# Score products of a sliding-window attention kernel at 128 columns where only 128 are read

## The chip, the cores and the metric

The kernel runs on one core of a Trainium2 chip. A core has TensorE (PE: matrix products; its weight loads are shown apart as PEld), VectorE (DVE), ScalarE (ACT), GpSimd (POOL) and SyncE (SP), which issues most transfers here. The metric is the time of one execution in device microseconds; lower is better.

## What is computed

The input has 2048 tokens of 512 values. Cut to what matters, with 32 heads of 16 values and a window of 256 tokens:

```
xn     = layernorm(x)
q,k,v  = split(xn @ wqkv)
scores = q @ k.T / 4, kept where 0 <= i - j < 256
s      = (softmax(scores) @ v) @ wo
g      = silu((silu(xn @ w_gate) * (xn @ w_up)) @ w_down)
out    = x + s * g
```

## The kernel before, in words

The tokens are worked in four chunks of 512. The dense products (projections `a`, values `vp`, gate and up `g`, `u`, down `d`, output `s`) split each fp32 operand into a high and a low part of type F32R (a 4-byte type that TensorE runs in its own way) and add three products, high by high, low by high and high by low. They contract over 64 rows at a time: the array is used as two halves, rows 0 to 63 and 64 to 127, and each half runs its own stream of products beside the other (`half(r)`).

Attention is worked in 32 units, 8 per chunk, each of four heads. In each unit the scores are computed twice:

- `max_pair` (line 955) makes a tile `b` for each of 16 pairs of head and block of 128 queries: queries by keys, 384 keys wide, or less in the first chunk, where the first two blocks of queries have only 128 and 256 keys behind them. VectorE (line 977) adds the mask and takes the maximum over the `n` columns that count. The product is `w` columns wide.
- `max_turn` turns the maxima, and they are added to the queries as one more row.
- `prob_pair` (line 1073) makes tiles `c`, keys by queries, in pieces that the function `pieces` lists. A piece is (key block, first query block, width `w`, first column in the bank `at0`, and the columns `v0` to `v1` of it that are used). ScalarE (line 1084) takes the exponential over the used columns, GpSimd masks the diagonal blocks.
- `pv_visit` (line 1140) multiplies the probabilities with the values on eight tiles of the array of 64 by 32. Its operands are plain F32, not F32R.

Here `b` and `c` have F32R operands (`qs` and `ks`), with 48 and 49 rows, one half of the array for each of two heads.

The order of the instructions of all engines is written out by a planner in the program: it keeps a clock for each half of TensorE (`issue`, line 1315, adds 0.000447 us per column and 0.004 us per product) and one for each other engine, and it puts attention work between dense products by due times that count finished dense work:

```
def issue(r, cols):
    front[0] = max(front[0], clock[r])
    clock[r] = front[0] + cols * 0.000447 + 0.004
```

On the chip the engines wait for one another by semaphores alone.

Of the kernel before, what the change touches and what calls it, by code (L numbers as in the profile page):

```python
# [54 lines left out]
def tile_window_attention_swiglu_gate(  # L55
# [27 lines left out]
    def sb(name, shape, dtype, kind, n):  # L83
        return pers.tile(shape, dtype, name=name, tag=ring(kind, n), bufs=1)
# [21 lines left out]
    def do(e, ready, cost, fn, then=None, slack=0.5, can=None, lat=None):  # L106
        seq[0] += 1
        queue[e].append((ready + slack, seq[0], ready, cost, fn, then, can, LAT.get(e, 0.0) if lat is None else lat))
# [67 lines left out]
    def bank(pool, name):  # L176
        tag = min((v, k) for k, v in pool.items() if v is not None)[1]
        pool[tag] = None
        return ps.tile([P, 512], F32, name=name, tag=tag, bufs=1), tag
# [775 lines left out]
    def max_pair(u, p, qb):  # L955
        c = u // NG
        lo = qb * P
        n = 3 * P
        if c == 0 and qb < 2:
            lo, n = HALO, (qb + 1) * P  # L960
        w = max(n, 256)
        m = mts[u % 2]
        for h in range(2):
            j = 2 * p + h
            r = R * h
            pb, tag = bank(rb_free, f"b{u}_{qb}_{j}")

            def go(pb=pb, r=r):
                nc.tensor.matmul(  # L969
                    pb[:, :w], qs[u % 3][r : r + 48, p, qb * P : (qb + 1) * P],  # L970
                    ks[u % 3][r : r + 48, p, lo : lo + w], start=True, stop=True,
                )

            def ttr(pb=pb, j=j):
                junk = sb(f"jk{u}_{qb}_{j}", [P, 3 * P], BF16, "jk", 1)
                col = 8 * (j % 2) + 4 * (j // 2) + qb
                nc.vector.tensor_tensor_reduce(  # L977
                    junk[:, :n], pb[:, :n], maskb[:, 3 * P - n :], 1.0, -3.0e38,
                    ALU.add, ALU.max, m[:, col : col + 1],
                )  # L980

            def after(t, tag=tag):
                rb_free[tag] = t
                ttr_at[u] = ttr_at.get(u, []) + [t]

            extra[h].append((w, go, lambda t, ttr=ttr, after=after: do("V", t, 0.23 + 0.00098 * n, ttr, after, 0.0)))
# [43 lines left out]

    def pieces(c, e):
        if c == 0:
            return ([(3, 2, 256, 0, 128, 256), (2, 2, 256, 256, 256, 512)],
                    [(0, 0, 384, 0, 0, 384)], [(1, 1, 384, 0, 0, 384)])[e]
        return ([(3, 2, 256, 0, 128, 256), (-2, 0, 256, 256, 256, 384)],
                [(-1, 0, 256, 0, 0, 256), (2, 2, 256, 256, 256, 512)],
                [(0, 0, 384, 0, 0, 384)], [(1, 1, 384, 0, 0, 384)])[e]

# [22 lines left out]
    def prob_span(u, e):  # L1061
        pcs = pieces(u // NG, e)
        return min(q[4] for q in pcs), max(q[5] for q in pcs)
# [9 lines left out]
    def prob_pair(u, e, p):  # L1073
        c = u // NG
        pcs = pieces(c, e)
        a, b = prob_span(u, e)
        if p == 0:
# [62 lines left out]
    def pv_visit(u, es):  # L1140
# [3 lines left out]
        for e in es:  # L1144
            for kb, qb, w, at0, v0, v1 in pieces(c, e):
                for r in range(2):
                    k64 = 2 * kb + r
                    a, b = max(k64, 0), min(k64 + 5, 8)
                    jobs[r].append((b - a, e, kb, R * a, R * b, at0 + R * a - P * qb))
# [57 lines left out]
    def plan_attention():  # L1207
        for u in range(NU):
            c = u // NG
            if u:  # L1210
                marks.append((u - 1 + 0.3, load_qk, (u,)))
            for n in range(8):
                streams[0].append((u + 0.02 + 0.1 * n, max_ready, max_pair, (u, n // 4, n % 4)))
            streams[0].append((u + 0.8, turn_ready, max_turn, (u, 0)))
            streams[0].append((u + 0.8, turn_ready, max_turn, (u, 1)))
            ne = 3 if c == 0 else 4
            for n in range(2 * ne):
                streams[1].append((u + 1.07 + 0.1 * n, prob_ready, prob_pair, (u, n // 2, n % 2)))
            streams[1].append((u + 1.89, pv_ready, pv_visit, (u, tuple(range(ne)))))
        for c in range(1, NCH):  # L1220
            marks.append((8 * c - 4.9, load_x, (c,)))
            for k in range(KC):
                streams[2].append((8 * c - 3.3 + 0.25 * k, xt_ready, xt_turn, (c, k)))
        for s in streams:
            s.reverse()
        marks.sort(key=lambda m: -m[0])
# [258 lines left out]
```

## Time and profile before

| | |
|---|---|
| time, median of 3 runs | 858.4 us (857.58 to 859.4) |
| time of the profiled execution | 858.88 us |
| its span, first to last instruction | 857.2 us |
| granted TensorE clock, mean | 0.999 |
| PE, PEld busy | 99%, 92% of the span |
| DVE, ACT, POOL busy | 57%, 58%, 70% of the span |

The time is the span and 1.7 us around it. A product's duration in the trace holds the time that it takes to pass through the array, so products that overlap are each shown longer than the distance between their starts. A busy TensorE is therefore not one at its peak; distances between starts say what a product costs.

### The profile page before, as it was taken

To read this page: it belongs to the slowest core of one execution; us is meant where nothing else is said; L and a number is where in the kernel's file an instruction comes from. 1 tells how busy PE (TensorE), PEld (TensorE's weight loads), DVE (VectorE), ACT (ScalarE), POOL (GpSimd) and SP (SyncE) were. 2 spreads that over 40 slices of the span, in tenths; PEclk is the share of its full clock that TensorE was granted. 3 is DMA by queue.
4 is the path that set the end of the run, shared out by engine and by line. 5 is a ranking of instruction groups with operands and counts; after the bars stand their busy time and mean duration, and the time that the engine had idled before them with its cause. 6 is when DMAs were issued, how large, how long until landed. Compare 5 with 4: busy or idle time off the path is not lost.

```text
span 857.2 us, 29679 instructions
## 1 busy us (share of the span) xinstructions
PE 851.1 (99%) x11960; PEld 792.0 (92%) x11960; DVE 485.9 (57%) x1633; ACT 495.9 (58%) x1056; POOL 597.3 (70%) x630
## 2 busy tenths in 40 slices
PE   9999999999999999999999999999999999999997
PEld 8999999999899898989899999899999989989897
DVE  4464566655656656755566755566556656554233
ACT  4445565555766566565576655555656765555632
POOL 6756565758885766666789685666658797769754
PEclk9999999999999999999999999999999999999999
DMA  5854645457667853455767686454656767634341
GB/s 177 218 163 140 198 119 173 132 161 176 181 170 208 267 146 112 134 155 130 209 171 198 188 205 182 122 164 113 179 128 176 200 181 233 170 98 137 101 138 63
DMA packets 67629, 139.59 MB, mean 163 GB/s; under 512 B 12690, under 2 KB 21394, under 8 KB 67492
## 3 DMA queue, kind: packets, MB, share of 16 engines
q1 hardware_dynamic: 67204, 137.17, 57.3%
q8 instruction: 94, 1.54, 0.8%
q10 hardware_dynamic: 288, 0.52, 0.2%
q14 instruction: 43, 0.35, 0.1%
HBM read 107.74 MB, written 29.62 MB: 160 GB/s over the span
## 4 chain that ended last, share of the span: by engine, by line
PE 97%; DMA 1%; DVE 1%; issue 0%; ACT 0%; SPq 0%; DVEq 0%; ACTq 0%
PE g L455 19%; PE u L455 18%; PE d L455 18%; PE a L455 11%; PE pv L1160 8%; PE c L1123 6%; PE s L455 5%; PE vp L455 5%; PE b L969 5%; PE warm L235 1%; DMA wr<-wdn 1%; PE xp L473 0%; DVE jk L977 0%; PE xp L340 0%; PE mt L1003 0%
## 5 line engine op out<-in xcount | busy, mean ns | idle before, releaser
L426 POOL TENSOR_TENSOR wl<-wr,wh 128x512 fp32r<-128x512 f32 x240 | 298.2, 1259 | 137.8 <-ACT wh L438 129.1
L977 DVE CUSTOM_DVE_ANT_0 jk<-b,maskb 128x384 bf16<-128x384 f32 (+2 forms) x512 | 271.4, 530 | 141.3 <-PE b L969 80.7
L1084 ACT ACTIVATE p<-c 128x384 f32<-128x384 f32 (+1 forms) x480 | 208.0, 498 | 93.0 <-PE c L1123 83.7
L455 PE MATMUL d<-wh,hh 64*128 64x256 f32 x1792 | 237.2, 279 | 0.0
L455 PEld LDWEIGHTS d<-wh,hh 64*128 64x128 f32 x1792 | 208.2, 186 | 1.3 <-issue 0.8
L455 PE MATMUL d<-wl,hh 64*128 64x256 f32 x896 | 190.8, 279 | 0.0
L438 ACT ACTIVATE wh<-wr 128x512 fp32r<-128x512 f32 x240 | 142.6, 620 | 81.6 <-PE u L455 24.7
L455 PE MATMUL g<-xh,wl 64*128 64x512 f32 x448 | 173.0, 395 | 0.5 <-issue 0.5
L455 PE MATMUL g<-xh,wh 64*128 64x512 f32 x448 | 173.1, 395 | 0.0
L455 PE MATMUL g<-xl,wh 64*128 64x512 f32 x448 | 173.0, 394 | 0.0
L455 PE MATMUL u<-xh,wl 64*128 64x512 f32 x448 | 171.9, 396 | 0.0
L455 PE MATMUL u<-xl,wh 64*128 64x512 f32 x448 | 171.2, 394 | 0.0
L455 PE MATMUL u<-xh,wh 64*128 64x512 f32 x448 | 171.2, 394 | 0.0
L455 PEld LDWEIGHTS d<-wl,hh 64*128 64x128 f32 x896 | 143.0, 186 | 0.3
L1097 POOL TENSOR_SCALAR_AFFINE_SELECT p<-p 128x512 f32<-128x512 f32 x128 | 81.1, 637 | 51.6 <-ACT p L1084 46.9
L969 PE MATMUL b<-k,q 48*128 48x384 f32 (+1 forms) x512 | 111.6, 334 | 0.0
L1123 PE MATMUL c<-q,k 49*128 49x384 f32 (+1 forms) x704 | 105.2, 304 | 0.1
L455 PE MATMUL a<-xh,wh 64*128 64x512 f32 (+1 forms) x264 | 90.4, 395 | 0.0
L455 PE MATMUL a<-xh,wl 64*128 64x512 f32 (+1 forms) x264 | 88.6, 386 | 0.0
L455 PE MATMUL a<-xl,wh 64*128 64x512 f32 (+1 forms) x264 | 88.3, 387 | 0.0
L455 PEld LDWEIGHTS g<-xl,wh 64*128 64x128 f32 x448 | 82.6, 186 | 2.9 <-issue 0.2
L455 PEld LDWEIGHTS g<-xh,wh 64*128 64x128 f32 x448 | 82.7, 186 | 2.6 <-issue 0.2
(102 smaller groups left out, 2020.5 us busy)
## 6 DMA issues: line engine op xcount, KB each, us to landing
wr<-wgu SPq DMA_DIRECT2D x56, 512.0 KB
k<-qkd SPq DMA_DIRECT2D x48, 192.0 KB
wr<-wqk SPq DMA_DIRECT2D x16, 512.0 KB
qkd<-qkh SPq DMA_DIRECT2D x32, 256.0 KB
qkd<-qkl SPq DMA_DIRECT2D x32, 256.0 KB
q<-qkd SPq DMA_DIRECT2D x64, 128.0 KB
wr<-wdn SPq DMA_DIRECT2D x16, 512.0 KB
od<-ev SPq DMA_DIRECT2D x32, 256.0 KB
```

The lines of the kernel that those rows point to most:

```text
L235: nc.tensor.matmul(wbank[:, : rhs.shape[-1]], warm, rhs, start=True, stop=True)
L426: nc.gpsimd.tensor_tensor(lo, raw[j][:, n], f32(hi), op=ALU.subtract)
L438: do("S", t, 0.13 + 0.00078 * m, lambda: nc.scalar.activation(hi, raw[j][:, n], AF.Copy), after_high, sl)
L455: return nc.tensor.matmul(pb, a, b, start=first, stop=last, skip_group_check=True)
L969: nc.tensor.matmul(pb[:, :w], qs[u % 3][r : r + 48, p, qb * P : (qb + 1) * P], ks[u % 3][r : r + 48, p, lo : lo + w], start=True, stop=True,)
L977: nc.vector.tensor_tensor_reduce(junk[:, :n], pb[:, :n], maskb[:, 3 * P - n :], 1.0, -3.0e38, ALU.add, ALU.max, m[:, col : col + 1],)
L1084: nc.scalar.activation(t[:, h, :], pc[:, a:b], AF.Exp, scale=DH ** -0.5)
L1097: nc.gpsimd.affine_select(s, s, [[0, 4], [1, P]], ALU.is_ge, 0.0, base=0, channel_multiplier=-1)
L1123: nc.tensor.matmul(pc[:, at0 : at0 + w], ks[u % 3][r : r + 49, p, k0 : k0 + P], qs[u % 3][r : r + 49, p, qb * P : qb * P + w], start=(i == ...
L1160: nc.tensor.matmul(pbs[r][0][32 * j : 32 * j + 32, q0:q1], vt[half(r), (4 * c + kb) % VT, VW * (4 * g + j) : VW * (4 * g + j) + 32], t[hal ...
```

## The change

The score products of which only 128 columns are read become 128 columns wide in place of 256. In `max_pair` that is the first block of queries in the first chunk. In `pieces` it is the piece of key block 3, which had computed query block 2 too and left it unread, and, from the second chunk on, that of key block -2. What is read, the number of products, their operands in SBUF and all other code stay. The planner is told the new widths, since `w` is what it gets.

```diff
@@ max_pair
-        w = max(n, 256)
+        w = n
@@ pieces
         if c == 0:
-            return ([(3, 2, 256, 0, 128, 256), (2, 2, 256, 256, 256, 512)],
+            return ([(3, 3, 128, 128, 128, 256), (2, 2, 256, 256, 256, 512)],
                     [(0, 0, 384, 0, 0, 384)], [(1, 1, 384, 0, 0, 384)])[e]
-        return ([(3, 2, 256, 0, 128, 256), (-2, 0, 256, 256, 256, 384)],
+        return ([(3, 3, 128, 128, 128, 256), (-2, 0, 128, 256, 256, 384)],
                 [(-1, 0, 256, 0, 0, 256), (2, 2, 256, 256, 256, 512)],
                 [(0, 0, 384, 0, 0, 384)], [(1, 1, 384, 0, 0, 384)])[e]
```

## Rows read from the trace of the kernel before

**Rows 1.** The page, its head and the busy time of TensorE.

```profile
span 857.2 us, 29679 instructions
...
PE 851.1 (99%) x11960; PEld 792.0 (92%) x11960; DVE 485.9 (57%) x1633; ACT 495.9 (58%) x1056; POOL 597.3 (70%) x630
```

**Rows 2.** The page, the chain that ended last, by engine and line.

```profile
PE 97%; DMA 1%; DVE 1%; issue 0%; ACT 0%; SPq 0%; DVEq 0%; ACTq 0%
PE g L455 19%; PE u L455 18%; PE d L455 18%; PE a L455 11%; PE pv L1160 8%; PE c L1123 6%; PE s L455 5%; PE vp L455 5%; PE b L969 5%; PE warm L235 1%; DMA wr<-wdn 1%; PE xp L473 0%; DVE jk L977 0%; PE xp L340 0%; PE mt L1003 0%
```

**Rows 3.** All waits: who waited for whom, us, times, longest us.

```profile
ACT p L1084 <- PE c L1123: 83.7, 98, 5.0
DVE jk L977 <- PE b L969: 80.7, 100, 4.2
```

**Rows 4.** The waits of TensorE's weight loads, same columns.

```profile
PEld pv L1160 <- issue: 4.9, 16, 0.4
PEld pv L1160 <- POOL p L1101: 2.2, 6, 0.4
...
PEld c L1123 <- ACT p L1084: 1.0, 4, 0.3
```

**Rows 5.** Groups by form, PE: xcount, busy us, mean ns, idle before.

```profile
L455 PE MATMUL g<-xh,wh 64*128 64x512 f32 x448 | 173.1, 395 | 0.0
...
L969 PE MATMUL b<-k,q 48*128 48x384 f32 x448 | 99.1, 341 | 0.0
...
L1123 PE MATMUL c<-q,k 49*128 49x384 f32 x256 | 53.8, 342 | 0.0
L1123 PE MATMUL c<-q,k 49*128 49x256 f32 x448 | 51.5, 283 | 0.1
...
L1160 PE MATMUL pv<-p,v 64*32 64x320 f32 x1024 | 41.8, 435 | 0.0
...
L1160 PE MATMUL pv<-p,v 64*32 64x128 f32 x448 | 13.4, 269 | 0.0
L969 PE MATMUL b<-k,q 48*128 48x256 f32 x64 | 12.4, 286 | 0.0
...
L1160 PE MATMUL pv<-p,v 64*32 64x64 f32 x448 | 11.2, 222 | 0.0
```

**Rows 6.** Timeline of PE, 405.3 to 407.5 us: start us, us, group.

```profile
405.41 0.41 PE L1123 MATMUL c<-q,k 49*128 49x256 f32 x4
405.65 0.40 PE L455 MATMUL a<-xl,wh 64*128 64x512 f32 x2
405.89 0.34 PE L969 MATMUL b<-k,q 48*128 48x384 f32 x2
406.07 0.40 PE L455 MATMUL a<-xh,wl 64*128 64x512 f32 x2
...
406.99 0.40 PE L455 MATMUL a<-xh,wh 64*128 64x512 f32 x2
407.23 0.40 PE L1123 MATMUL c<-q,k 49*128 49x256 f32 x4
407.47 0.40 PE L455 MATMUL a<-xl,wh 64*128 64x512 f32 x2
```

**Rows 7.** Timeline of PE, 401.3 to 403.5 us.

```profile
401.64 0.28 PE L455 MATMUL d<-wl,hh 64*128 64x256 f32 x2
...
403.35 0.28 PE L455 MATMUL d<-wl,hh 64*128 64x256 f32 x2
```

**Rows 8.** Groups by form, PEld (the weight loads).

```profile
L1123 PEld LDWEIGHTS c<-q,k 49*128 49x128 f32 x704 | 78.0, 186 | 4.7 <-ACT p L1084 1.0 <-DVE m L977 0.5
...
L1160 PEld LDWEIGHTS pv<-p,v 64*32 64x32 f32 x2816 | 50.3, 106 | 26.7 <-issue 4.9 <-POOL p L1101 2.2 <-DVE m L977 0.4
```

**Rows 9.** The longest pieces of the chain: start us, us, what.

```profile
399.11 2.38 PE pv L1160 x93
```

## The prediction

> **What bounds the kernel now.** I read the head of the page first, then the chain of work that ended last, then the waits, and only then single products. TensorE is busy for 851.1 of 857.2 us [rows 1]; that alone says little, since overlapping products are shown longer than they cost. The chain says more: 97% of the span is TensorE, and the lines that the change touches, `c` (L1123) and `b` (L969), hold 6% and 5% of it [rows 2]. The waits point the same way. The two readers of the scores sit idle until TensorE delivers: ScalarE 83.7 us for `c`, VectorE 80.7 us for `b` [rows 3], while the largest waits on TensorE's own side are a few us over the whole run [rows 4]. So nothing covers a score product: whatever one of them costs in its half of the array, more or less, goes into the time.
>
> **How many products change.** From the code: in `max_pair`, the first of four query blocks for 4 heads in the 8 units of the first chunk, 32 products. In `pieces`, one piece for 4 heads in those 8 units, 32, and two pieces for 4 heads in the 24 other units, 192. Together 256, all from 256 to 128 columns. The trace agrees with this reading of the code: it has 448 `c` of 256 columns (64 in the first chunk, 384 after) and 64 such `b` [rows 5]; half of each is to change. Two heads run side by side on the two halves, so 128 changes lie behind one another in each half. The price wanted is that of one product in its half, times 128.
>
> **What one costs now.** Distances between starts, not durations. Four `c` of 256 columns, two in each half, start at 405.41 and the next product at 405.65; again at 407.23 and 407.47 [rows 6]: 0.24 us for two, 120 ns each. Dense products of 256 columns: from 401.64 to 403.35 there are 15 in each half, 114 ns each [rows 7]. A `b` of 384 takes 0.18 us (405.89 to 406.07), and five products of 512 from 406.07 to 407.23, of which the last starts at 406.99, take 230 ns each (0.92 us over four) [rows 6]. So from 256 columns up the cost is about 0.45 ns a column ((230 - 114) / 256) and nearly nothing besides.
>
> **What 128 columns cost: the unknown.** No F32R product here is narrower than 256, so the price has to be bounded from both sides.
>
> From below: if the line goes on, 0.45 ns by 128 columns and the few ns that a `c` has over a dense product give about 62 ns, 58 ns less than now.
>
> From above: the nearest rows of 128 columns and less are `pv`, with F32 operands. The code issues 1408 of them (48 in each of 24 units, 32 in each of 8) and the trace has 2816 of their weight loads [rows 8]: each runs as two recorded products, each with a load of its own, while `c` has one load for each of its 704. Within `pv`, a record gets longer by 0.83 ns a column ((435 - 222) / 256) against 0.44 for F32R ((395 - 283) / (512 - 256)) [rows 5]. Both together, twice the records at nearly twice the time, make F32 about four times as dear: 2 by 0.83 by 128 is 213 ns. The other way, a visit of `pv` from the second chunk on runs 5+5+4+3+2+1 blocks of 64 columns on each tile, 1280 columns, in 2.38 us [rows 9], 1.86 ns a column or 238 ns for 128. If TensorE treats a narrow F32R product like F32, one costs 213 to 238 ns, 93 to 118 ns more than now.
>
> In between lies what I take. Each product loads its own 128 columns of weights. Only the next set can be loaded ahead: I read that from the structure of the stream (one load for every product) and treat it as an assumption. Then a product can't follow the one before it sooner than a load takes. How long is that? The duration of a load is no better than that of a product, but its growth with size should be as good: for `pv`, the same growth of durations gave 0.83 ns a column and the distances of a whole visit, over two records, 0.93. Loads of 32 columns take 106 ns and of 128 columns 186 [rows 8], 0.83 ns a column, so the 128 columns hold the loading path for about 107 ns. That is nearly the 107 ns by which 256 moving columns at 0.42 ns (2.4 GHz, the level granted here) hold the other path. A 256-column product and its successor's load are in balance now. At 128 columns the products get shorter and the loads don't. The cost would stay between 107 ns and today's 120; with the 6 to 13 ns that products of 256 show over their columns, 113 to 120. I take 117, as the overhead seems to belong to each pair of load and product: 3 ns saved by 128 is 0.4 us, and 0 to 0.9 us for the two ends.
>
> There is a rule that speaks against this. The rows say 114 to 120 ns for 256 columns with loads that grow by 0.83 ns a column [rows 6 to 8]. The Trainium skill, in "TensorE: Matmul & The Clock Gate", section "Back-to-back issue gap", gives about 81 ns for a product of 128 columns in a stream of pairs of load and product, and says both set the distance. By it the sum would be 128 by (120 - 81), 5.0 us gained, where my reading of the rows gives 0.4. It does not say for which type; no run here shows one.
>
> **The rest of the edit.** The readers take the same columns: 128, 256, 384 and 512 in L977 and L1084, unchanged, and they wait for TensorE anyway [rows 3]. No DMA, no semaphore wait and no load is added or taken away. What does move is the planner's clock: it books 57 ns less for each narrow product, 7.3 us per half over the run, spread evenly. Attention work is placed by finished dense work, which does not change; engine and bank times are compared with the shorter clock, so some instructions can change places. Where the chip takes longer than the plan, the other engines have more time than planned, not less. With waits of this size on TensorE's side [rows 4] I put this at 0, with 1.5 us either way.
>
> **The sum.** The profiled execution took 858.88 us, its span 857.2. Less 0.4: 858.5. Against the median of the runs, 858.4, 0.5 below the profiled one: 858.0. What a measurement of this kernel can tell from no change is about 0.2%, 1.7 us.
>
> **The rivals.**
>
> *Narrow F32R falls to the pace of F32 (slower).* Place: all 256 products, on TensorE's path. For it: F32 in the same trace does cost four times as much a column [rows 5, 9], F32R is a faster way to run the same 4-byte data, and every F32R product in the trace has at least 256 columns, so nothing shows that the faster way holds below. Against it: nothing in the trace shows a price that jumps with width; `pv` durations go in even steps from 222 at 64 to 269 at 128 and 435 at 320 [rows 5]. Price: 93 to 118 ns by 128, 11.9 to 15.1 us; 870.3 to 873.5, middle 871.9, 1.6% slower. It decides the sign as soon as a narrow product costs more than 120 + 13 ns (1.7 us over 128).
>
> *The load does not bind (faster).* Then the column line holds: 58 ns by 128 is 7.4 us, 851.0. For it: the start of each product well before the recorded end of its load (186 ns against distances of 114 [rows 7, 8]) shows that loads overlap more than their records say. Against it: the growth by 0.83 ns a column. A load that takes half of what I read would give a cost between, and a gain of 2 to 7 us. The page named above would put its 5.0 us gain here.
>
> *The planner's shorter clock changes the order for the worse.* A late `c` or `p` makes TensorE wait. For it: waits of 0.3 to 0.4 us at single visits exist [rows 4]. Against it: they are few. One such wait in every one of the 32 units would be 10 to 13 us; I see room for about one in eight, 1.6 us, and give little to more than that.
>
> **How the numbers follow.** Load-bound, nearly nothing: 0.50. As dear as F32: 0.34. Load does not bind: 0.12. The order, by over 0.2% in either direction: 0.04. The predicted time is that of the likeliest, 858.0; its own range with 1.5 us for the order is 856.4 to 859.7. The second case is too likely to be left out, so the range goes up to the end of it, 873.6, and down to 856.2, and leaves out mainly the third. Faster by over 0.2%: the third case and a part of the first and fourth, 0.17. Slower: the second and a small part of the others, 0.39. Within: 0.44.
>
> **What the profile after would show.** Right: 224 `c` and 32 `b` of 128 columns, one record each; four narrow `c`, two in each half, still take about 0.23 us from their first start to the next product's, and their loads still 186 ns; the narrow records themselves are shorter than 283 ns, near 225, though the pace is the same. Wrong in the one way: twice as many records of 128 columns, or the same number at a distance of 210 ns and more, with busy time of `c` and `b` and the span up by 12 to 15 us. Wrong in the other: four narrow `c` in 0.12 to 0.16 us, and the span down by 5 us or more. If the waits of PEld for POOL or ACT grow by some us while the distances stay, it was the order.

## The result: slower by 3.6 us

The changed kernel takes 861.97 us (median of 5 runs, 861.81 to 862.16) against 858.37 for the kernel before (5 runs): ratio 1.0042, 95% interval 1.0027 to 1.0056. It is slower, and by more than a measurement can miss. That the time lies in the range of the prediction is luck: the forecast was no change, with 859.7 us as its own upper end, the range went up to 873.6 for the rival of F32's pace alone, and that rival is not what happened.

The page of the changed kernel, its head and busy time, as in [rows 1], and its chain, as in [rows 2]:

```profile
span 860.2 us, 29688 instructions
...
PE 854.6 (99%) x11960; PEld 799.0 (93%) x11960; DVE 487.1 (57%) x1633; ACT 496.8 (58%) x1056; POOL 597.0 (69%) x630
...
PE 98%; DVE 0%; DMA 0%; ACT 0%; POOL 0%; issue 0%; POOLq 0%; DVEq 0%; ACTq 0%
```

The span grew by 3.0 us, the number of products and loads is the same, 11960 each, and TensorE still is the chain. So no narrow product became two records (F32 products do, as the prediction counted on `pv`). The groups by form of the score products and of their loads, as in [rows 5, 8] (xcount, busy us, mean ns, idle before):

```profile
L1123 PE MATMUL c<-q,k 49*128 49x256 f32 x224 | 30.5, 290 | 0.2
L1123 PE MATMUL c<-q,k 49*128 49x128 f32 x224 | 24.1, 246 | 0.0
...
L969 PE MATMUL b<-k,q 48*128 48x256 f32 x32 | 6.3, 284 | 0.0
...
L969 PE MATMUL b<-k,q 48*128 48x128 f32 x32 | 5.3, 225 | 0.0
```

```profile
L1123 PEld LDWEIGHTS c<-q,k 49*128 49x128 f32 x704 | 82.3, 185 | 2.8 <-ACT p L1084 0.6
...
L969 PEld LDWEIGHTS b<-k,q 48*128 48x128 f32 x512 | 72.4, 184 | 3.2 <-ACT p L1084 0.3 <-DVE m L977 0.2 <-issue 0.2
```

224 `c` and 32 `b` are 128 wide, as counted, their records are shorter (246 and 225 ns, against 290 and 284 for 256 columns), and their loads take 185 and 184 ns, where they took 186 and 185. No narrow product is shown longer than a wide one. The second thing that the change does is to tell the planner the new widths, and with that the order of TensorE's instructions differs soon after the first score products. These two had to be told apart.

### The profile page after: what moved, and what is told of

Its sections match the earlier page's. It is cut to its first block, busy times and chain, and to the rows that moved or that the text cites. A ratio compares the mean times of both kernels' runs of the same rounds, so it can differ in the third digit from the quotient of the medians.

```text
span 860.2 us, 29688 instructions
## 1 busy us (share of the span) xinstructions
PE 854.6 (99%) x11960; PEld 799.0 (93%) x11960; DVE 487.1 (57%) x1633; ACT 496.8 (58%) x1056; POOL 597.0 (69%) x630
## 4 chain that ended last, share of the span: by engine, by line
PE 98%; DVE 0%; DMA 0%; ACT 0%; POOL 0%; issue 0%; POOLq 0%; DVEq 0%; ACTq 0%
PE g L455 19%; PE u L455 19%; PE d L455 19%; PE a L455 11%; PE pv L1160 8%; PE c L1123 5%; PE s L455 5%; PE vp L455 5%; PE b L969 5%; DMA xt<-x 0%; PE xp L473 0%; PE xp L340 0%; ACT p L1084 0%; POOL oh L905 0%; PE mt L1003 0%
## 5 line engine op out<-in xcount | busy, mean ns | idle before, releaser
L455 PE MATMUL d<-wh,hh 64*128 64x256 f32 x1792 | 233.9, 280 | 0.1
L455 PEld LDWEIGHTS d<-wh,hh 64*128 64x128 f32 x1792 | 203.7, 185 | 2.0 <-issue 0.8
L455 PE MATMUL d<-wl,hh 64*128 64x256 f32 x896 | 187.0, 280 | 0.0
L455 PE MATMUL g<-xh,wh 64*128 64x512 f32 x448 | 176.6, 397 | 0.0
L455 PE MATMUL u<-xl,wh 64*128 64x512 f32 x448 | 173.9, 396 | 0.0
L455 PE MATMUL u<-xh,wh 64*128 64x512 f32 x448 | 173.9, 395 | 0.0
L455 PEld LDWEIGHTS d<-wl,hh 64*128 64x128 f32 x896 | 139.2, 185 | 0.3
L1097 POOL TENSOR_SCALAR_AFFINE_SELECT p<-p 128x512 f32<-128x512 f32 x128 | 81.1, 637 | 58.9 <-ACT p L1084 54.1
L969 PE MATMUL b<-k,q 48*128 48x384 f32 (+2 forms) x512 | 113.2, 331 | 0.0
L455 PE MATMUL a<-xl,wh 64*128 64x512 f32 (+1 forms) x264 | 90.4, 388 | 0.0
L455 PEld LDWEIGHTS g<-xh,wl 64*128 64x128 f32 x448 | 82.9, 185 | 2.4
```

The source lines that it names most:

```text
L455: return nc.tensor.matmul(pb, a, b, start=first, stop=last, skip_group_check=True)
L969: nc.tensor.matmul(pb[:, :w], qs[u % 3][r : r + 48, p, qb * P : (qb + 1) * P], ks[u % 3][r : r + 48, p, lo : lo + w], start=True, stop=True,)
L1097: nc.gpsimd.affine_select(s, s, [[0, 4], [1, P]], ALU.is_ge, 0.0, base=0, channel_multiplier=-1)
```

## Experiments: the price of a product, and the order

Theory A: a narrow product costs about what a wide one does, since its load binds, and the 3.6 us are the new order. Theory B: the narrow products themselves cost 28 ns more each (3.6 us over 128).

**narrow_old_order** is the changed kernel with the old booking (the booking is the width that the planner counts for a product), so that all TensorE products stand in the order of the kernel before:

```diff
-            extra[h].append((w, go, ...))        # in max_pair and prob_pair
+            extra[h].append((max(w, 256), go, ...))
```

> The products are 128 columns wide as in the change, but the planner still books 256 columns for them, so that every engine's instructions stand in the order of the kernel before. Theory A (a narrow product costs as much as one of 256 because its weight load binds, and the 3.6 us of the changed kernel come from the order that the planner's shorter clock makes): 857.5 to 859, no different from before. Theory B (the narrow products themselves cost more on TensorE, 3.6 us over 128 in each half, 28 ns each): about 862.

Measured: 857.54 us against 858.64, ratio 0.9989 (0.9980 to 0.9998).

**wide_new_order** is the kernel before with the booking of the changed one:

```diff
-            extra[h].append((w, go, ...))        # max_pair
+            extra[h].append((n, go, ...))
-                extra[h].append((w, go, ...))    # prob_pair
+                extra[h].append((v1 - v0, go, ...))
```

> The products stay 256 columns wide, but the planner books 128 columns for those that the change narrows, so that the instructions stand in the order of the changed kernel. Theory A (the order): about 862, as the changed kernel. Theory B (the narrow product's own price): about 858.4, as before.

Measured: 862.88 against 858.64, ratio 1.0056 (1.0043 to 1.0069).

B falls and A stands: with the old order the narrow products gain about 1 us, and with the old products the new order alone loses 4.2 us. The changed kernel's 3.6 us are the sum of the two, within the noise.

**wo_in_halves** prices 128 columns by themselves, on dense products:

```diff
+                            cut = 2 if isinstance(self, Wo) else 1
+                            wide = 256 // cut
+                            for s in range(cut):
                                 mm(pb[:, t*256 + wide*s : ... + wide], self.act(k, a)[half(r), tok],
                                    w[k // 2][b][half(r), k % 2, wide*s : ... + wide], ...)
```

> Every dense product of the output projection (768 of 256 columns, 384 in each half of the array) is run as two of 128 columns, each with its own weight load, order otherwise as before. It prices 128 columns by itself. If the load binds at about 117 ns, each pair costs 234 in place of 114 ns: 46 us more, about 904. If narrow F32R products go at the pace of F32 (213 to 238 ns each): 120 to 139 us more, 978 to 997. If the load does not bind (62 ns): 4 us more, 862.

Measured: 902.22 against 858.64, 43.6 us more; over 384 that is 113.5 ns for the added product, with the whole difference put down to it. That is neither the pace of F32 nor 62 ns. Timeline of PE in a stretch of these products:

```profile
885.16 0.27 PE L455 MATMUL s<-wh,xl 64*128 64x128 f32 x1
885.16 0.27 PE L455 MATMUL s<-wl,xh 64*128 64x128 f32 x1
885.27 0.27 PE L455 MATMUL s<-wh,xl 64*128 64x128 f32 x2
885.38 0.27 PE L455 MATMUL s<-wh,xh 64*128 64x128 f32 x1
885.38 0.27 PE L455 MATMUL s<-wh,xl 64*128 64x128 f32 x1
```

Both halves start a product every 0.11 us. Over all these products the median distance between starts in a half is 112 ns; dense products of 256 columns in the kernel before have 118, so the 114 of [rows 7] is at the low end. It fits a load that binds, and equally a narrow product that streams at half the pace.

**wo_in_quarters** (`cut = 4`) tells these two apart.

> Every dense product of the output projection (384 in each half) as four of 64 columns in place of one of 256, each with its own load of 128 weight columns. The halves cost 227.5 ns a pair, 114 each, which fits a load that binds, and as well a narrow F32R product that streams at twice the time a column (2 x 0.42 x 128 = 107 ns). If the load binds, the price does not fall with the width: 4 x 114 for 114 ns, 131 us more, about 990. If it is the stream at twice the time, 64 columns cost some 60 ns: 4 x 60 for 114, 48 us more, about 907.

Measured: 1171.55 us in the profiled run; a second run took 4472 us, of which there is no profile and no explanation. Even the first is far from both numbers. The stretches at the end of the profiled run show why; timeline of PE (start us, us, group), then two windows (PE and PEld busy, and after the engines the granted clock):

```profile
1083.63 0.72 PE L455 MATMUL s<-wl,xh 64*128 64x64 f32 x8
1084.08 0.72 PE L455 MATMUL s<-wh,xl 64*128 64x64 f32 x8
1084.52 0.72 PE L455 MATMUL s<-wh,xh 64*128 64x64 f32 x8
1084.97 0.72 PE L455 MATMUL s<-wl,xh 64*128 64x64 f32 x8
...
1099.80 1.25 PE L455 MATMUL s<-wl,xh 64*128 64x64 f32 x8
1100.65 1.25 PE L455 MATMUL s<-wh,xl 64*128 64x64 f32 x8
1101.50 1.25 PE L455 MATMUL s<-wh,xh 64*128 64x64 f32 x8
```

```profile
1083.60:1085.30 1.70, 1.70 (x34) 1.70 (x34) 0.55 (x1) 1.64 (x4) 1.70 (x3) 1.00 0.00 0
1090.00:1165.00 75.00, 75.00 (x685) 75.00 (x685) 4.85 (x14) 0.00 (x0) 0.00 (x0) 0.50 0.04 12
```

At full clock eight products, four in each half, take 0.447 us (1083.63 to 1084.97 for three such groups): 112 ns each at 64 columns, as at 128. Halving the width took nothing off, so the price is not the stream's. Nor is it the issuing of loads and products: in `pv`, whose loads are 32 columns wide, 93 such pairs take 2.38 us [rows 9], 26 ns each over both halves, where these take 56. What is left is what a load of 128 columns takes in its half. How much of that is its columns and how much a fixed time was not tested, as no F32R product here loads fewer. In the second window the granted clock is 0.50 (1.2 GHz), and eight products take 0.85 us, 213 ns each. That makes up the rest of the time, by an estimate: a mean granted clock of 0.847 over 1169.8 us means some 358 us at half the clock, half of them lost, 179 us; with the 131 us expected of the load this is 310 of the 313 us that the run took longer.

How the load binds is seen in one place of narrow_old_order against the same place before, both in the same order. Timeline of PEld, first before, then narrow_old_order:

```profile
697.16 0.43 PEld L1123 LDWEIGHTS c<-q,k 49*128 49x128 f32 x4
697.52 0.18 PEld L455 LDWEIGHTS u<-xl,wh 64*128 64x128 f32 x1
697.52 0.19 PEld L455 LDWEIGHTS g<-xh,wl 64*128 64x128 f32 x1
697.64 0.19 PEld L455 LDWEIGHTS g<-xh,wh 64*128 64x128 f32 x1
697.64 0.19 PEld L455 LDWEIGHTS u<-xh,wl 64*128 64x128 f32 x1
```

```profile
696.81 0.42 PEld L1123 LDWEIGHTS c<-q,k 49*128 49x128 f32 x4
697.16 0.19 PEld L455 LDWEIGHTS u<-xl,wh 64*128 64x128 f32 x1
697.16 0.19 PEld L455 LDWEIGHTS g<-xh,wl 64*128 64x128 f32 x1
697.27 0.19 PEld L455 LDWEIGHTS u<-xh,wl 64*128 64x128 f32 x1
697.27 0.19 PEld L455 LDWEIGHTS g<-xh,wh 64*128 64x128 f32 x1
```

Timeline of PE at that place, two lines of before, then narrow_old_order:

```profile
697.39 0.41 PE L1123 MATMUL c<-q,k 49*128 49x256 f32 x4
697.64 0.39 PE L455 MATMUL u<-xl,wh 64*128 64x512 f32 x1
```

```profile
697.04 0.34 PE L1123 MATMUL c<-q,k 49*128 49x128 f32 x4
697.22 0.44 PE L455 MATMUL u<-xl,wh 64*128 64x512 f32 x1
697.22 0.44 PE L455 MATMUL g<-xh,wl 64*128 64x512 f32 x1
697.50 0.38 PE L455 MATMUL u<-xh,wl 64*128 64x512 f32 x1
```

From the first load of `c` to the loads two places after `c` it is 0.48 us before and 0.46 us with narrow products, about 10 ns less for each of the two narrow products in a half: loads follow one another at 0.11 us, where they followed wide products at 0.12. Before, the load of the next product starts as a product starts (both at 697.64), so here one load runs ahead and no more. Looking at products alone misleads here: the next one starts 0.18 us after the first `c` (0.25 before), which looks like the 62 ns of the column line; but its successor then starts after 0.28 us in place of 0.23. A product's start is recorded ahead of the end of its load (`u` at 697.22, its load from 697.16 on for 0.19 us). Taken from the start before the narrow products to the second one after them, all places of the two runs give 7 to 8 ns less for each (median), 0.9 to 1.0 us over 128.

**wide_booked_250** and **wide_booked_255** ask whether it is the size of the wrong booking that harms, or any other order. Products as before, booked a little short:

```diff
-            extra[h].append((w, go, ...))        # in max_pair and prob_pair
+            extra[h].append((w if w > 256 else 250, go, ...))   # 255 in the other
```

> Everything as before, but the planner books 250 columns for the score products of 256: 3 ns less each, which changes nothing that matters in the planner's picture but lets its ties and orders fall otherwise. If any change of order scatters the time by some us (theory A as a lottery), it is off from 858.4 by 1 us or more to either side. If only the large error of 57 ns a product does harm, it stays within 858.4 +- 0.9.

Measured: 862.99 against 858.64, ratio 1.0054 (1.0041 to 1.0066).

> All products as before, booked at 255 columns in place of 256, 0.45 ns less each. If only a large error of the booking harms, 858.6, as before. If the order is a draw, off by some us: the planner's own clock ends 2.5 us later than for the kernel before, 859.7 against 857.3, so about 861.2.

Measured: 861.80 against 858.93, ratio 1.0045 (1.0028 to 1.0062). A booking that is wrong by 0.45 ns a product costs 2.9 us, one wrong by 57 cost 4.2 (the intervals of the ratios overlap): the size of the error hardly matters, the order that falls out does.

**wide_booked_128_first_chunk** and **wide_booked_128_later_chunks** split the booking of the change (`v1 - v0 if c == 0 else w`, and the reverse; `b` is booked short in the first only).

> All products 256 wide as before; the planner books 128 columns for those of the first chunk alone (32 of the 128 in each half). If the harm grows with the sum of the wrong booking, a quarter of what wide_new_order lost: 859.7. If any change of order is a draw that the planner's own clock foresees: that clock, with the 1.8 us that it does not book put back, ends at 865.1 against 857.3 for the kernel before, so about 866.

Measured: 865.93 against 858.12, ratio 1.0092 (1.0077 to 1.0107). A quarter of the wrong booking loses more than all of it, 7.8 us against 4.2.

> All products 256 wide as before; the planner books 128 columns for those of the second to fourth chunk alone (96 of the 128 in each half). By the sum of the wrong booking: three quarters of the loss, 862. By the planner's own clock with 5.5 us put back, 859.2 against 857.3: about 860.5.

Measured: 861.26 against 858.12, ratio 1.0038 (1.0024 to 1.0052).

**narrow_booked_240** books the narrow products at what they cost (`max(w, 240)`).

> The changed kernel with the narrow products booked at 240 columns in the planner (111 ns, about what the load-to-load distance of narrow products showed) in place of 128 (61 ns). If only the wrong booking of 57 ns a product did the harm, 857.5: before, less 0.9. If any other order is a draw between about -1.5 and +5 us, it can land anywhere there; the planner's own clock ends at 857.4 for it (857.3 for the kernel before), which would make it 858 to 859.

Measured: 858.17 against 858.93, ratio 0.9993 (0.9984 to 1.0002): no difference that shows.

**wide_booked_267** and **narrow_booked_267** (`w if w > 256 else 267`, without and with the narrow products) take an order that the planner's own clock calls better.

> All products as before, the 256-column score products booked at 267 columns. By the planner's own clock this order is better than that of the kernel before by 1.6 us (856.9 with 1.3 us of the overbooking to be taken off, against 857.3): about 857.0. If the kernel before has the best order there is and any other loses, 859 to 863.

Measured: 858.98 against 858.93, ratio 1.0000 (0.9990 to 1.0009). The gain of 1.6 us did not come; nor is the kernel before the best order that exists by much.

> The same order as the one before it in this list, with the products narrowed to 128 columns as in the change. If the narrow products' own worth is the 0.9 us that both earlier pairs showed, and adds to the order's, 856.1, which would be faster than both kernels by 2.5 and 6 us. If it does not add, as wide_booked_267.

Measured: 857.17 against 858.93, ratio 0.9985 (0.9976 to 0.9995). It is faster than both kernels, by 0.15% and, by the two ratios, 0.6%. The forecast of 856.1 was missed, since the order's gain did not come. By the ratios the narrow products are worth 1.3 us here, 0.9 in the old order and 1.2 in the new one, each uncertain by 1 us or more; the traces of all three pairs show 7 to 8 ns a product (median), 0.9 to 1.0 us over 128.

Six orders of the same wide products, against the planner's own clock (its end when the program is built, with 0.447 ns put back for each column booked short or taken off for each booked over; 857.3 for the kernel before):

```
booking                  planner   measured
128 (wide_new_order)       +5.9      +4.2 us
250                        +5.1      +4.4
255                        +2.6      +2.9
267                        -1.6       0.0
128, first chunk           +7.9      +7.8
128, later chunks          +1.9      +3.1
```

The planner's clock knows the order's price to about 2 us. The orders that small edits draw lie mostly some us above that of the kernel before.

## Where an order loses its time

The waits of TensorE's loads stay as small as in [rows 4]; the largest of the changed kernel, same columns:

```profile
PEld pv L1160 <- issue: 4.2, 15, 0.4
PEld pv L1160 <- POOL p L1101: 2.7, 7, 0.5
```

TensorE runs two streams, one in each half, and the views count it as busy when either runs. Timeline of PE in the changed kernel:

```profile
235.30 0.39 PE L455 MATMUL u<-xh,wl 64*128 64x512 f32 x1
235.41 0.39 PE L455 MATMUL g<-xh,wl 64*128 64x512 f32 x1
235.53 0.39 PE L455 MATMUL u<-xh,wh 64*128 64x512 f32 x1
235.76 0.39 PE L455 MATMUL u<-xl,wh 64*128 64x512 f32 x1
...
237.13 0.39 PE L455 MATMUL u<-xl,wh 64*128 64x512 f32 x1
237.36 0.39 PE L455 MATMUL u<-xh,wl 64*128 64x512 f32 x1
237.37 0.43 PE L1123 MATMUL c<-q,k 49*128 49x128 f32 x2
```

Up to 235.4 `u` and `g` alternate, one in each half. Then nine `u` follow one another at 0.23 us, all in one half, and the other has nothing until `c` at 237.37: 1.7 us of half an engine. The program has them so: these nine and three `g` of the same half stand in a row in it. In the views TensorE is busy throughout (20.00 of 20.00 us from 220 to 240). A second place, the chain of the changed kernel from 262 to 272 us:

```profile
by line: PE s L455 17.8%; PE a L455 17.6%; ACT p L1084 14.5%; PE vp L455 13.8%; POOL oh L905 13.0%; PE c L1123 10.1%; issue 5.7%; PE b L969 5.0%; ACT qkh L549 1.9%; POOLq L426 0.3%; ACTq L1084 0.2%; ACTq L438 0.2%
```

There the score products come with no dense work between them, and the chain runs through ScalarE's exponentials and GpSimd's `oh`: 27% of 10 us outside TensorE.

With each product put to its half by the program's order, I summed the distances between starts of F32R products in a half beyond 230, 176, 116 and 113 ns for 512, 384, 256 and 128 columns. Of single holes (such an excess of over 250 ns) the kernel before has 14 with 7.5 us over both halves and narrow_old_order 13 with 9.0; in the new order wide_new_order has 21 with 11.9 and the changed kernel 22 with 12.5. All excess together grew from 53.8 us before to 58.9 in wide_new_order, 61.6 in wide_booked_250 and 63.4 in wide_booked_128_first_chunk: 2.6, 3.9 and 4.8 us a half, where 4.2, 4.4 and 7.8 us were measured. So these distances account for some 60 to 90% of the order's price; where the rest lies is not shown. Why the planner leaves a half empty at just these places was not followed further.

## Why the prediction was wrong, by its steps

- What bounds the kernel, and the count of 256 products, 128 in each half: as predicted.
- The price of a narrow product: the mechanism was right, the load binds, at 112 ns, and the size was a little off: 117 ns taken, so 3 ns saved, for what the traces show as 7 to 8 ns, 0.9 to 1.0 us over 128, at the upper end of the term's 0 to 0.9 us. The times alone, 1.1 us and uncertain by 0.8, can't tell that from the 0.4 us forecast. The assumption that only one load runs ahead holds in what the traces show.
- "With waits of this size on TensorE's side [rows 4] I put this at 0, with 1.5 us either way": **this is the step that failed**. The term of the planner's clock measured +4.2 us. The argument before it, that the chip's other engines only get more time, answers the wrong question: the program's order itself gives one half nothing to do, as from 235.4 us on, or has score products without dense work beside them, as from 264 us on, where the halves wait for ScalarE and GpSimd. [Rows 1, 2 and 4] can't show either, as they count either half's work as TensorE's.
- The rival of F32's pace: refuted by one record each, and by 113.5 ns in wo_in_halves. The slower sign had a chance of 0.39, nearly all of it for this wrong reason.
- The rival that the load does not bind: refuted by 112 ns at both 128 and 64 columns. The Trainium skill, "TensorE: Matmul & The Clock Gate", section "Back-to-back issue gap", has about 81 ns at 128 columns; for these 4-byte operands the runs show 112, and the measurement decides.
- The rival of the order had the right place and too small a size, "about one in eight, 1.6 us", and a chance of 0.04. It counted waits that stop all of TensorE, of which there are few, and no empty halves.
- What the profile after would show: counts, single records and loads as said; the narrow records took 246 ns (`c`) and 225 (`b`) for "near 225". The distance of 0.23 us from the first narrow `c` to the next product was 0.18 in narrow_old_order, and would have spoken against the load: its cost appears one product later. The sign given for the order, waits of PEld for POOL or ACT that grow by some us, did not come (2.2 to 2.7 us and 1.0 to 0.6), and yet it was the order.

## What to carry to other kernels

A product that loads its own 128 weight columns had a floor of 112 ns here at full clock, so cutting an F32R product from 256 to 128 columns gained 7 to 8 ns and not half of it. Where a program computes its own order from booked costs, a change of width is two changes; run each alone, with the old booking and with the old widths, before either gets the blame. Where two halves of the array run two streams, a busy share of 99% can hide an empty half: read the starts in each half.

## What was not expected of the hardware

TensorE's granted clock fell to 0.50 (1.2 GHz) during long stretches of 64-column products, while loads and products ran back to back and the engine was shown busy all the time (75.00 of 75.00 us). The same loads with 128 columns, in wo_in_halves, kept it at 0.999 over the run. The price of a 64-column product rose from 112 to 213 ns with it.
